# The last 512 tokens of a sliding-window attention: sums transposed straight into the projection's tile, and the load of two constant matrices issued earlier in the spectral layer that follows

## The chip, the cores and the metric

The kernel runs on one core of one Trainium2 chip, with its tensor engine (PE; PEld is its weight load), vector engine (DVE), scalar engine (ACT), GpSimd (POOL) and sync engine (SP, which here only issues DMAs). The metric is the time of one execution in microseconds of the device; a lower time is better.

## The reference

The input is 2048 tokens of 576 numbers in float32. Two layers alternate, twice each:

```
x = x + A(layernorm(x));  x = x + B(layernorm(x));  x = x + A(layernorm(x));  x = x + B(layernorm(x))

A: q, k, v = x @ wqkv  (32 heads of 18)
   p = softmax(q k^T / sqrt(18)) over the 256 newest tokens up to the query's own
   A = (p v, heads side by side) @ wo
B: X = rfft2(x) * (w_r + i w_i);  B = irfft2(X)
```

The weights are the same in both rounds. So the program holds the code of an attention layer and of a spectral layer twice, in what is called here the first and the second half.

## The kernel before, in words

Matrix products are made in a split form: a number is held as a high and a low part, and three products (high by high, low by high, high by low) replace one. Nothing is scheduled by a tool: each engine runs its instructions in the order in which the Python code writes them, and waits on semaphores. SP is one such queue: a DMA that waits for something holds up every DMA that is written behind it. A DMA also takes one of eight semaphores in turn, and waits until the DMA that last had that semaphore has landed.

**Attention.** The 32 heads are worked in eight groups of four (`n`), and each group's 2048 tokens in 16 blocks of 128; a counter `t` runs over the 128 blocks. Scores go through PSUM tiles `S` and `E`, ACT makes the exponentials (tile `P`), POOL masks them, and `pv` (L830) adds them up, by matrix products with the values, into the PSUM tile `U`: a head's 18 sums and, as the 19th row, the sum of its exponentials. Every fourth block ACT copies `U` to `us` (L835). `norm(n, c)` (L836 to L850) then turns the 512 tokens of chunk `c` on their side (four transposes `tpo`, L840), divides by the 19th column (L843, L845) and writes the result to DRAM: columns 0 to 447 of a token into `o_d`, columns 448 to 575 into `o7_d`. Group 7 has columns 504 to 575, group 6 columns 432 to 503.

**Projection.** The class `Out` multiplies by `wo` and adds the input. It works in 16 *units*: unit `u` is the tokens `16 p + u`, one for each partition `p`. So the last 512 tokens are partitions 96 to 127 of every unit. `load(u)` fetches a unit's first 448 columns (into `o`, three buffers) and its input (into `x`, five buffers); `tail(u)` splits 64 of the columns on POOL; `turn(u)` transposes them (L506, L507) and copies them out of PSUM; `early(u)` makes the 22 products that need only these columns (L529), `late(u)` the six that need columns 448 to 575, and the sum with the input (two DVE additions, L551), and stores it. These last columns of all units are in one SBUF tile `o7` of 128 partitions by 16 units by 128 columns, which `last` fetches from `o7_d` (L497); `turn_last` transposes one unit's part (L518, PSUM tile `tpl`), `split_last` copies and splits it (L523 on ACT, L524 on DVE, into `oL`). Units 0 to 2 have their early products while the attention ends. `sums(u)` (L558 to L560) and `stats(u)` (L564, L565) make the next layer's layernorm of a unit.

**Spectral layer.** It has three stages. The first, per unit: `f0` normalises (ACT `xn`, L163) and folds the row (POOL, `eo`, `tl`); `f1` transposes (PSUM `tp`, one buffer, shared with the projection's `turn`) and splits it (`et`, L184 on ACT, L185 on DVE, L186 on ACT); `f2` makes the transform along the row (`pf`, L196), `f3` the first part of that along the tokens (`pz`, L209; copied to `ye` by DVE, L211). Units 3 to 15 of the projection are written in between. `norm(u)`, another function of this name, is `sums` and `f0` of a unit. `f3` writes `ye` to DRAM (`yd`, L223). The last three sets of tokens (`n2` of 13, 14, 15) also go by small SBUF-to-SBUF DMAs (L222) into the first tile of the second stage, whose other rows are read back from `yd` (L215). The second stage works in 16 groups `g`: read two groups' rows from `yd` (L264), multiply (`p`, L276), weigh (DVE L280 to L282, POOL L284, L285), multiply back (`pq`, L295), copy (`ze`, L297), store (L309). Its group 0 needs the rows sent by L222, its group 2 a read of `yd` after the write of all 16 sets. The third stage transforms back with two constant matrices, `ga` and `ic` (0.5 and 1.7 MB), which L219 and L218 load into SBUF over the projection's `wo` and transposed tiles; three small memsets (L217) clear the padding of its `z` tiles there.

## Time and profile before

| | |
|---|---|
| time, median of 3 runs | 1618.0 us (1613.05 to 1623.72) |
| the profiled execution: its own time | 1615.73 us |
| its span | 1614.0 us |
| mean granted clock of the tensor engine | 0.974 |
| PE busy | 1514.2 us, 94% of the span |
| DVE, ACT, POOL busy | 976.2, 813.7, 626.0 us |
| attention ends, projection begins | 512 to 540 us (first half), 1321 to 1349 us (second) |
| second stage of the spectral layer begins | 676.2 us, 1484.6 us |

How to read what follows: a row of the timeline has the start, the duration, engine, line, operation, `out<-in`, shapes and count, and in square brackets how long the engine idled before it and what ended that. A row of the chain of waits has start, duration, engine and line; "SPq" is SP's queue. A row of windows has, for a stretch, busy time and count per engine, the granted clock of PE (1.00 is full), the mean busy share of the DMA engines and GB/s. DMAs that write `o7_d` are shown as `o_d`, those that read it as `ofree<-o_d`; `ofree` is the SBUF area that holds `o`, `x`, `o7` and the second stage's tiles, `oroom` the one of `wo`, the transposed tiles, `ic` and `ga`.

### The profile page before, as it was taken

How to read it: one execution, taken by the hardware profiler on the slowest of the kernel's cores; microseconds unless marked ns; L12 is line 12 of the kernel's file. 1: busy time of each engine (PE TensorE's matmuls, PEld its weight loads, DVE VectorE, ACT ScalarE, POOL GpSimd, SP SyncE). 2: the span in 40 equal slices, each digit the busy share in tenths (PEclk: the TensorE clock that was granted, in tenths of full speed). 3: DMA queues.
4: the chain of work that ended last, by engine and by line, in shares of the span. 5: the costliest groups of instructions: out<-in, count | busy, mean ns of one | idle time of the engine just before them, and what ended most of it. 6: DMA issues, size and time to landing. Idle time of an engine off the chain costs nothing.

```text
span 1614.0 us, 38199 instructions
## 1 busy us (share of the span) xinstructions
PE 1514.2 (94%) x13872; PEld 1145.7 (71%) x13872; DVE 976.2 (60%) x3141; ACT 813.7 (50%) x1900; POOL 626.0 (39%) x1028
## 2 busy tenths in 40 slices
PE   7999999999999899789879999999999998997898
PEld 7975666666656799648879756666666567996498
DVE  4337777777773455356743367777777744554567
ACT  5424666666676344224445146666666773442243
POOL 2172344444455233152411723444343552431524
PEclk9999999999999999898989999999999999998999
DMA  6656456555444456666474563554444444666664
GB/s 204 173 184 209 135 151 188 151 164 149 151 126 135 130 186 193 204 208 213 145 229 111 190 209 121 153 152 138 134 131 146 127 133 120 194 197 198 220 212 140
DMA packets 187881, 268.46 MB, mean 166 GB/s; under 512 B 86830, under 2 KB 91950, under 8 KB 186670
## 3 DMA queue, kind: packets, MB, share of 16 engines
q1 hardware_dynamic: 179374, 246.03, 49.7%
q10 hardware_dynamic: 7680, 15.59, 2.7%
q0 software_dynamic: 640, 4.39, 1.0%
q8 instruction: 111, 1.82, 0.5%
q14 instruction: 76, 0.62, 0.1%
HBM read 167.00 MB, written 102.29 MB: 167 GB/s over the span
## 4 chain that ended last, share of the span: by engine, by line
PE 79%; DMA 8%; ACT 3%; DVE 2%; issue 1%; SPq 1%; POOL 1%; POOLq 0%; ACTq 0%; DVEq 0%
PE pj L741 17%; PE E L814 14%; PE U L830 12%; PE S L782 7%; PE ops L529 6%; PE vps L699 4%; PE pi L340 3%; PE pz L209 3%; PE po L361 3%; PE pf L196 3%; DMA yd<-ze 3%; PE tpo L840 2%; DMA o_d<-o 1%; ACT P L815 1%; PE po L365 1%
## 5 line engine op out<-in xcount | busy, mean ns | idle before, releaser
L784 DVE CUSTOM_DVE_ANT_0 jk<-S,mask 128x384 bf16<-128x384 f32 (+2 forms) x1024 | 500.4, 529 | 155.5 <-PE S L782 143.3
L815 ACT ACTIVATE P<-E 128x384 f32<-128x384 f32 (+2 forms) x1024 | 426.2, 471 | 209.5 <-PE E L814 179.4
L817 POOL TENSOR_SCALAR_AFFINE_SELECT P<-P 128x512 f32<-128x512 f32 x256 | 163.0, 637 | 454.1 <-ACT P L815 437.6
L814 PE MATMUL E<-qs,ks 64*128 64x384 f32 (+2 forms) x1024 | 269.1, 433 | 12.3 <-ACT P L815 11.5
L814 PEld LDWEIGHTS E<-qs,ks 64*128 64x128 f32 x1024 | 129.2, 184 | 156.2 <-ACT P L815 93.3
L782 PE MATMUL S<-ks,qs 63*128 63x384 f32 (+2 forms) x1024 | 228.6, 351 | 0.1
L830 PE MATMUL U<-P,vq 128*19 128x128 f32 x5760 | 209.7, 277 | 0.1
L830 PEld LDWEIGHTS U<-P,vq 128*19 128x19 f32 x5760 | 137.2, 99 | 57.2 <-issue 53.9
L741 PE MATMUL pj<-xh,wqh 128*128 128x512 f32 x360 | 153.6, 427 | 1.8 <-ACT vt L703 1.7
L782 PEld LDWEIGHTS S<-ks,qs 63*128 63x128 f32 x1024 | 130.7, 188 | 24.8 <-DVE m L784 13.3
L820 POOL TENSOR_SCALAR_AFFINE_SELECT P<-P 128x512 f32<-128x512 f32 x224 | 142.6, 637 | 0.0
L741 PE MATMUL pj<-xh,wql 128*128 128x512 f32 x360 | 123.7, 418 | 0.0
L529 PE MATMUL ops<-oroom 128*128 128x288 f32 x784 | 114.7, 303 | 5.1 <-DVE oroom L512 3.0
L741 PE MATMUL pj<-xl,wqh 128*128 128x512 f32 x288 | 119.1, 414 | 0.0
L529 PEld LDWEIGHTS ops<-oroom 128*128 128x128 f32 x784 | 107.1, 192 | 7.4 <-DVE oroom L512 4.0
L340 PE MATMUL pi<-oroom 128*128 128x256 f32 (+1 forms) x576 | 78.5, 293 | 15.6 <-ACT oroom L325 15.6
L745 DVE TENSOR_TENSOR sg<-pj,sg 128x512 fp32r<-128x512 f32 x72 | 49.8, 692 | 70.0 <-ACT sg L744 65.0
L741 PEld LDWEIGHTS pj<-xh,wqh 128*128 128x128 f32 x360 | 67.5, 188 | 33.6 <-issue 21.7
L340 PEld LDWEIGHTS pi<-oroom 128*128 128x128 f32 (+1 forms) x576 | 74.6, 191 | 17.2 <-ACT oroom L325 16.5
L784 DVE DVE_READ_ACCUMULATOR2_ANT m<- 128x1 f32 x1024 | 85.3, 83 | 0.0
L741 PEld LDWEIGHTS pj<-xh,wql 128*128 128x128 f32 x360 | 64.0, 188 | 27.1 <-issue 17.7
L165 POOL TENSOR_TENSOR eo<-xn 128x287 f32<-128x287 f32 x32 | 26.1, 817 | 146.5 <-ACT xn L163 135.4
(165 smaller groups left out, 2562.5 us busy)
## 6 DMA issues: line engine op xcount, KB each, us to landing
qk_d<-sg SPq DMA_DIRECT2D x56, 512.0 KB
qs<-qk_d SPq DMA_DIRECT2D x384, 72.0 KB
ks<-qk_d SPq DMA_DIRECT2D x384, 72.0 KB
v_d<-vt SPq DMA_DIRECT2D x32, 304.0 KB
vq<-v_d SPq DMA_DIRECT2D x16, 608.0 KB
yd<-ye SPq DMA_DIRECT2D x32, 290.0 KB
wt<-in_w SPq DMA_DIRECT2D x16, 580.0 KB
x<-ofree SPq DMA_DIRECT2D x32, 288.0 KB
```

The lines of the kernel that those rows point to most:

```text
L340: T.matmul(o, z[:, sl, c, lo:lo + m], mo, start=k == 0, stop=k == 5)
L529: self.nc.tensor.matmul(self.ps[u][n][:, 0:288], x, self.w[p][:, wk * D + n * 288:wk * D + n * 288 + 288], start=first and i == 0, stop=la ...
L699: T.matmul(ps[:, n, 0:288], xT(xk, c), w[:, wk, n * 288:(n + 1) * 288], start=i == 0, stop=i == len(ks) - 1)
L741: T.matmul(box["ps"], w[:, wk], xT(xk, cs), start=s == 0, stop=s == len(ks) - 1)
L745: V.tensor_sub(sg[:, 1], box["ps"], sg[:, 0].bitcast(F32))
L782: T.matmul(ps[:, 0:N], q[b:b + 63, pair, i * 128:i * 128 + 128], k[b:b + 63, pair, lo:hi], start=True, stop=True)
L784: V.tensor_tensor_reduce(out=jk[:, 0:N], in0=ps[:, 0:N], in1=mask[:, 384 - N:384], scale=1.0, scalar=-3e38, op0=ALU.add, op1=ALU.max, accu ...
L814: T.matmul(ps[:, 0:nq], k[b:b + 64, pair, j * 128:j * 128 + 128], q[b:b + 64, pair, j * 128:j * 128 + nq], start=True, stop=True)
L815: A.activation(p[:, hl_, 0:nq], ps[:, 0:nq], AF.Exp, scale=SC)
L817: P.affine_select(out=p[:, :, 0:128], in_=p[:, :, 0:128], pattern=[[0, 4], [1, 128]], compare_op=ALU.is_ge, fill=0.0, base=0, channel_mult ...
L820: P.affine_select(out=p[:, :, 256:384], in_=p[:, :, 256:384], pattern=[[0, 4], [-1, 128]], compare_op=ALU.is_gt, fill=0.0, base=0, channel ...
L830: T.matmul(U[32 * h:32 * h + 19, (i % 4) * 128:(i % 4) * 128 + 128], vts[n][:, j, h], pt[n, j][:, h, (i - j) * 128:(i - j) * 128 + 128], s ...
```

## The change

It has four parts.

1. The last `norm` of the attention, that of group 7 and the last 512 tokens, is no longer made by four 128x128 transposes, a store and a load. Sixteen transposes take every 16th column of `us`, so that each gives the 32 tokens of one unit on 32 partitions (`tpz`); four pairs of DVE instructions on 32 partitions divide and write `o7` directly. `last` now has a column range: rows 96 to 127 of group 6's 56 columns are fetched behind the constants, and rows 0 to 95 two steps before the counter ends.
2. The `norm` of chunk 2 of group 7 is written one block earlier. `turn_last` and `split_last` of units 0 to 2 are written ahead of the early products of unit 2 instead of behind the turn of unit 3.
3. At the start of the spectral layer `load(6)`, `load(7)`, `tail(6)` and `tail(7)` are written earlier, `norm(2)` ahead of `f1(0)`, and `norm(4)` ahead of `f3(0)`.
4. The memsets and the loads of `ic` and `ga` are taken out of `f3` of set 13 and written behind `f1` of set 12, after the projection's last unit.

```diff
@@ in f3
                 nc.sync.dma_start(y_tile(0)[0:8 * FD].rearrange("p a c f -> p a (c f)"), yd[0][0:2, 0:FD].rearrange("a n i f -> (n i) a f"))
-                for z in zs:
-                    V.memset(z.bitcast(F32)[:, :, :, 289:320], 0.0)
-                nc.sync.dma_start(ic.rearrange("p a f -> p (a f)").bitcast(F32), ic_d.rearrange("p a f -> p (a f)").bitcast(F32))
-                nc.sync.dma_start(ga.rearrange("p a j c -> p (a j c)").bitcast(F32), ga_d.bitcast(F32))
@@ the spectral layer's first stage
         norm(1)
+        out.load(6)
         out.tail(5)
         out.unit(3, pp)
+        norm(2)
+        out.load(7)
+        out.tail(6)
         f1(0, hs[0])
-        norm(2)
         out.unit(4, pp)
         f2(0, hs[0])
         out.ahead(5, pp)
         norm(3)
+        out.tail(7)
         for t in range(1, NT - 4):
...
             if t == 1:
+                norm(4)
                 f3(0, hs[0])
                 out.ahead(6, pp)
-                norm(4)
...
         f1(NT - 4, hs[NT - 4])
+
+        for z in zs:
+            V.memset(z.bitcast(F32)[:, :, :, 289:320], 0.0)
+        nc.sync.dma_start(ic.rearrange("p a f -> p (a f)").bitcast(F32), ic_d.rearrange("p a f -> p (a f)").bitcast(F32))
+        nc.sync.dma_start(ga.rearrange("p a j c -> p (a j c)").bitcast(F32), ga_d.bitcast(F32))
@@ Out
-    def last(self, r):
-        self.nc.sync.dma_start(self.o7[r], self.o7v[r])
+    def last(self, r, c):
+        self.nc.sync.dma_start(self.o7[r, :, c], self.o7v[r, :, c])
...
-        if u < NT - 1:
+        if 7 <= u < NT - 1:
             self.load(u + 1)
             self.tail(u + 1)
@@ the attention's end
-                y = t - 4
-                if 0 <= y < NX and y % 4 == 3:
+                y = t - 3 if t == NX - 2 else t - 4
+                if 0 <= y < NX - 1 and y % 4 == 3 and (t != NX - 1):
                     due.append((norm, *divmod(y // 4, 4)))
...
                     out.consts()
+                    out.last(slice(96, 128), slice(0, 56))
+                if t == NX - 1:
+                    out.last(slice(0, 96), slice(0, 128))
...
-            out.last(slice(0, 96))
             out.early(0, [pp.tile([128, 512], F32, tag="S", name=f"ops0_{n}", bufs=3) for n in range(2)], slice(0, 4))
-            norm(NQ - 1, 3)
-            out.last(slice(96, 128))
+
+            for k in range(4):
+                tp = pp.tile([128, 512], F32, tag=("pj", "E")[k // 2], name=f"tpz{k}", bufs=2)[0:32]
+                for a in range(4):
+                    T.transpose(tp[:, 128 * a:128 * a + 128], us[NQ - 1, 3][:, 4 * k + a:512:16], ident)
+                tv = tp.rearrange("p (a h e) -> p a h e", a=4, h=4)
+                rc = wp.tile([128, 4, 4, 1], F32, tag="rc", name=f"rcz{k}", bufs=2)[0:32]
+                V.reciprocal(rc, tv[:, :, :, 18:19])
+                V.tensor_mul(out.o7[96:128, 4 * k:4 * k + 4, 56:128].rearrange("p a (h e) -> p a h e", e=18), tv[:, :, :, 0:18],
+                             rc.to_broadcast([32, 4, 4, 18]))
             out.early(0, None, slice(4, 11))
             out.early(1, ...)
-            out.early(2, ...)
-            out.turn(3, U, A)
-            out.tail(4)
             tp = pp.tile([128, 512], F32, tag="pj", name="tpl", bufs=2)
             for f in (out.turn_last, out.split_last):
                 for u in range(3):
                     f(u, tp[:, 128 * u:128 * u + 128])
+            out.early(2, ...)
+            out.turn(3, U, A)
+            out.tail(4)
```

Three places show what moves. The first is PE's order at the end of the attention, where the last columns of units 0 to 2 are transposed (`tpl`); `ops_S`, `ops_E` are unit 1's early products, `ops_E` with `ops_pj` unit 2's, `U` here is the turn of unit 3. Before:

```order
L529 MATMUL ops_E<-oroom 128x288
L529 MATMUL ops_pj<-oroom 128x288
L506 MATMUL U<-ident,ofree 128x128 x3
L507 MATMUL U<-ident,ofree 128x128
L518 MATMUL tpl<-ident,ofree 128x128 x3
```

And of the change:

```order
L534 MATMUL ops_S<-oroom 128x288
L534 MATMUL ops_E<-oroom 128x288
L523 MATMUL tpl<-ident,ofree 128x128 x3
L534 MATMUL ops_E<-oroom 128x288
L534 MATMUL ops_pj<-oroom 128x288
```

The three transposes now stand between the early products of units 1 and 2, with 22 products and the turn of unit 3 behind them; before, they stood behind all of these.

The second is DVE's order at the start of the spectral layer, from the additions of unit 3 (`ops_8535`, in the change `ops_8559`) to those of unit 4; `et` is the split of `f1(0)`, the rows from BN_STATS to SCALAR_TENSOR_TENSOR are the layernorm of unit 2. Before:

```order
L551 TENSOR_TENSOR ofree<-ofree,ops_8535 128x288 x2
L185 TENSOR_TENSOR et_8574<-tp_8567,et_8574 128x2x256
L558 BN_STATS ofree<-ofree 128x6 x2
L559 BN_AGGR ofree<-ofree 128x2
L564 RECIPROCAL ofree<-ofree 128x1
L565 SCALAR_TENSOR_TENSOR ofree<-ofree 128x1
L551 TENSOR_TENSOR ofree<-ofree,ops_8593 128x288 x2
```

And of the change:

```order
L556 TENSOR_TENSOR ofree<-ofree,ops_8559 128x288 x2
L563 BN_STATS ofree<-ofree 128x6 x2
L564 BN_AGGR ofree<-ofree 128x2
L569 RECIPROCAL ofree<-ofree 128x1
L570 SCALAR_TENSOR_TENSOR ofree<-ofree 128x1
L185 TENSOR_TENSOR et_8617<-tp_8610,et_8617 128x2x256
L556 TENSOR_TENSOR ofree<-ofree,ops_8621 128x288 x2
```

The four rows of unit 2's layernorm now stand ahead of `et`; on ACT the root, `xn` and the copy to `eo` of unit 2 stand ahead of `et`'s two copies in the same way. One step later the layernorm of unit 4 has moved ahead of the copy `ye` and of unit 6's copies in the same manner.

The third is SP's queue at the end of the spectral layer's first stage. `yd<-ye` are the stores of sets 10, 11, 12 and on, `icr` and `gar` the two constant matrices, `ofree<-yd` the read into the first tile, `ofree<-ye` the small DMAs of set 13. Before:

```order
L223 DMA yd_8484<-ye_9830 16x8x580
L143 DMA wt_9920<-in_w 128x2x580
L223 DMA yd_8484<-ye_9918 16x8x580
L156 DMA m_8496<-in_m 128x1024
L223 DMA yd_8484<-ye_9966 16x8x580
L215 DMA ofree<-yd_8484 104x2x580
L218 DMA oroom<-icr 128x3480
L219 DMA oroom<-gar 128x1024
L222 DMA ofree<-ye_10013 8x580 x2
```

And of the change:

```order
L219 DMA yd_8506<-ye_9852 16x8x580
L260 DMA oroom<-icr 128x3480
L261 DMA oroom<-gar 128x1024
L143 DMA wt_9947<-in_w 128x2x580
L219 DMA yd_8506<-ye_9945 16x8x580
L156 DMA m_8518<-in_m 128x1024
L219 DMA yd_8506<-ye_9993 16x8x580
L215 DMA ofree<-yd_8506 104x2x580
L218 DMA ofree<-ye_10040 8x580 x2
```

The two loads have moved ahead by four DMAs and the read: a load of weights, two stores of `ye`, and the load of `m`.

## The prediction
> **What bounds the kernel now.** I read the page first, then the chain of waits at the two places that the change touches, then the timelines of single engines there and the windows with the granted clock.

> ```profile
> PE 1514.2 (94%) x13872; PEld 1145.7 (71%) x13872; DVE 976.2 (60%) x3141; ACT 813.7 (50%) x1900; POOL 626.0 (39%) x1028
> ```

> PE is busy for 94% of the span, so a microsecond is to be had only where PE stands still or runs at half clock. At the end of the attention the chain of waits of the first half is

> ```profile
> 523.44 5.64 DMA o_d<-o
> 529.10 3.13 DMA ofree<-o_d
> ```

> that is: the last chunk is stored, and then its rows are read back. PE's timeline shows how much of it PE feels, DVE's what follows:

> ```profile
> 529.10 0.49 PE L506 MATMUL U<-ident,ofree 128*128 128x128 f32 x3
> 529.42 0.27 PE L507 MATMUL U<-ident,ofree 128*128 128x128 f32 x1
> 532.48 0.52 PE L518 MATMUL tpl<-ident,ofree 128*128 128x128 f32 x3 [2.78 <-DMA ofree<-o_d]
> 539.71 3.99 PE L529 MATMUL ops<-oroom 128*128 128x288 f32 x28 [1.27 <-DVE oroom L512]
> ...
> 562.87 0.52 PE L506 MATMUL tpo<-ident,ofree 128*128 128x128 f32 x3 [2.07 <-DMA ofree<-o_d]
> ```

> ```profile
> 530.35 0.56 DVE L512 TENSOR_TENSOR oroom<-U,oroom 128x384 fp32r<-128x384 f32 x1 [8.03 <-ACT oroom L511]
> ...
> 534.79 0.81 DVE L551 TENSOR_TENSOR ofree<-ofree,ops 128x288 f32<-128x288 f32 x2
> ```

> The second half stands the same way:

> ```profile
> 1341.20 0.52 PE L518 MATMUL tpl<-ident,ofree 128*128 128x128 f32 x3 [2.83 <-DMA ofree<-o_d]
> ...
> 1371.70 0.52 PE L506 MATMUL tpo<-ident,ofree 128*128 128x128 f32 x3 [2.06 <-DMA ofree<-o_d]
> ...
> 1376.79 0.33 PE L179 MATMUL tp<-ident,eo 128*128 128x128 f32 x1 [0.25 <-DVE oroom L524]
> ```

> At the second place, the step from the spectral layer's first stage to its second, PE stands longer:

> ```profile
> 676.20 4.13 PE L276 MATMUL p<-ofree,fc 128*64 128x290 f32 x16 [6.60 <-DMA ofree<-ye]
> 680.26 1.42 PE L295 MATMUL pq<-uv,m 64*128 64x290 f32 x8
> 683.97 2.15 PE L276 MATMUL p<-ofree,fc 128*64 128x290 f32 x8 [2.29 <-DMA ofree<-yd]
> ...
> 1484.61 4.13 PE L276 MATMUL p<-ofree,fc 128*64 128x290 f32 x16 [7.26 <-DMA ofree<-ye]
> 1488.68 1.69 PE L295 MATMUL pq<-uv,m 64*128 64x290 f32 x8
> 1491.75 1.20 PE L276 MATMUL p<-ofree,fc 128*64 128x290 f32 x8 [1.39 <-DMA ofree<-yd]
> ```

> From the last `ye` on, the chain there is a small DMA, SP's issue, the store of set 15, and the read of groups 2 and 3:

> ```profile
> 670.43 5.30 DMA ofree<-ye
> 675.75 0.58 SPq L223
> 676.44 3.16 DMA yd<-ye
> ...
> 1478.19 5.82 DMA ofree<-ye
> ```

> The small DMA moves 18 KB and takes 5.30 us, in the second half (the last row) 5.82. What holds it and its neighbours is seen on SP: `ic` is issued six microseconds ahead of it, and SP itself waits for it (semaphores are taken in turn), with the stores of sets 14 and 15 queued behind:

> ```profile
> 664.76 0.34 SPq L218 DMA_DIRECT2D oroom<-icr  x1
> ```

> ```profile
> SPq L222 <- DMA oroom<-icr: 3.2, 1, 3.2
> ```

> **Part by part: `ic` and `ga` earlier.** What the small DMA costs alone is seen a stage later, where rows of `ze` go the same way:

> ```profile
> 725.58 0.56 SPq L305
> ```

> ```profile
> 728.73 0.67 ACT L325 CAST oroom<-ofree 128x578 fp32r<-128x578 f32 x1 [6.12 <-DMA ofree<-ze]
> ```

> The last one is issued at 725.58 and its reader runs at 728.73: 3.1 us. I take this; the other bound is today's 5.30. Set 15's leaves at 670.43, so group 0 starts at 673.5 and not at 676.20. From there to the end of the first `pq` it is 681.68 - 676.20 = 5.5 us, which places group 2 at 679.0. The other thing group 2 needs is the read:

> ```profile
> 667.92 0.76 DVE L211 COPY ye<-pz 128x580 f32<-128x580 f32 x1
> ```

> Set 14 is ready at 668.68. SP then issues two small DMAs (0.56 each) and set 14's store (0.58), so set 15's store starts at 670.4 where it started at 676.44; 6.0 us earlier, the read lands for a start at 678.0. The later of the two, 679.0, counts: 5.0 us in the first half. In the second, group 0 starts at 1478.19 + 3.1 = 1481.3, and to the end of `pq` it is 1490.37 - 1484.61 = 5.8, so group 2 stands at 1487.1 and not at 1491.75: 4.65. Bounds per half: nothing (the small DMA still takes 5.3) and 6.0 (the read alone sets it). The second stage goes on in steps that PE and the stores set, so I let the gain pass through whole. **Sum -9.65.**

> The loads themselves now run from about 649. The cover is

> ```profile
> 649.00:664.00 15.00, 13.34 (x101) 12.89 (x100) 6.77 (x10) 6.64 (x13) 2.24 (x5) 1.00 0.47 141
> ```

> DMA engines are 53% idle over these 15 us. The 2.3 MB, issued at 664.76 today, have landed when the small DMA has, at 675.73: 11 us at most, so by 660. Queued behind on SP stand a load of weights, the stores of sets 11 and 12, a load of `m` and the read of the first tile, which today goes just ahead of 664.76; so I let nothing there turn late. The three memsets sit on DVE, 55% idle over that window (6.77 of 15): nothing.

> **The join.** Removed: PE's wait of 2.78 us. Added on PE ahead of the turn of unit 3: 16 transposes less 4, and the three of `tpl`. Three transposes take 529.42 - 529.10 = 0.32, 0.11 each; 15 make 1.65. Their stationary operand now steps by 16 numbers, for which no row exists; bounds 0.09 (a shorter weight load) and, from the slowest row of its kind, below among the rivals. The four DVE pairs handle 288 numbers per partition each, as one of L551's two additions does in 0.4; 0.8 for a pair makes 3.2, beside 36 products of units 0 and 1 at 3.83/28 = 0.137 (unit 3's row less its drain), 4.9. The splits of `tpl` lie beside the 22 of unit 2. So L512 on `U` ends at 530.91 + 1.65 = 532.56, and with it the additions of unit 0 may start, which started at 534.79. From there to unit 3 the chain is DVE's own (additions, statistics, additions, turn of unit 4) and keeps its 4.92 us: unit 3 starts 2.2 us earlier. **-4.5 for both halves**; bounds 2.8 and nothing per half.

> PE then stands, between the late products and unit 3, for about 2.7 us with four transposes in it, longer than today's 1.27. What such a stretch costs:

> ```profile
> 533.90:537.30 3.40, 3.32 (x14) 2.96 (x14) 2.83 (x10) 0.82 (x5) 0.00 (x0) 0.50 0.23 87
> 564.50:567.90 3.40, 3.40 (x17) 3.40 (x16) 1.52 (x3) 2.22 (x5) 3.27 (x9) 0.52 0.10 37
> 1373.00:1376.40 3.40, 3.40 (x27) 3.30 (x25) 1.35 (x3) 2.35 (x5) 3.27 (x8) 1.00 0.24 88
> ```

> After the gap of 2.78 the clock is at half for 3.4 us (at 533.90, hidden there behind DVE); after 2.07 in the first half too (564.50), after 2.06 in the second not (1373.00). I take one halving in the two halves, at unit 3, 3.4 us at half speed: **+1.6**; bounds 0 and 3.2. [...]

> **The start of the spectral layer.** Two layernorms are put ahead of copies that PE waits for.

> ```profile
> 545.62 0.81 DVE L558 BATCH_NORM_STATS2 ofree<-ofree 128x6 f32<-128x288 f32 x2
> 547.91 0.97 PE L196 MATMUL pf<-dc,et 128*128 128x290 f32 x6
> 548.34 0.20 ACT L166 COPY eo<-xn 128x2 f32<-128x2 f32 x1
> ```

> A layernorm from its statistics to the copy of `eo` takes 548.54 - 545.62 = 2.9 us, ACT and DVE in turn. Today only the additions of unit 3 stand between that unit's end (543.70) and `et` of set 0. Now it is 0.81 for them, 2.9, and 0.6 and 0.7 for ACT's and DVE's part of `et` (as in the rows further down): 5.0 us, under a cover of 4.2 (547.91 - 543.70, unit 4). DVE's part is 0.8 late, ACT's, with which `pf` begins, 0.1: I take 0.65 per half, **+1.3**; bounds 0.1 and 0.8. Behind it stand `yh` of set 0 and unit 5's copies on the same engines.

> ```profile
> 556.99 0.69 DVE L185 TENSOR_TENSOR et<-tp,et 128x512 fp32r<-128x512 f32 x1 [0.46 <-ACT et L184]
> 558.95 0.59 ACT L511 CAST oroom<-tpo 128x512 fp32r<-128x512 f32 x1 [0.86 <-PE tpo L509]
> 560.46 0.29 DVE L524 TENSOR_TENSOR oroom<-tpo,oroom 128x128 fp32r<-128x128 f32 x1 [0.33 <-ACT oroom L523]
> ```

> `load(7)`'s wait, 2.07 and 2.06, goes away with its tail's 0.16, since SP issues it behind `xn` of unit 2, ten microseconds ahead of need. Next late is the one PSUM buffer `tp`: unit 6's copies, which started at 558.95, now stand behind unit 4's layernorm: 557.68 + 2.9 = 560.6, 1.65 later, and end at 562.4 instead of 560.75. So the turn of unit 7 moves from 562.87 only to 562.4: with the 0.16, 0.6 per half, **-1.2**. The wait of 0.25 for the next `tp` grows to about 0.7 in the second half, **+0.45**. In the first half it is hidden today under the half clock of unit 6:

> ```profile
> 563.75 5.49 PE L529 MATMUL ops<-oroom 128*128 128x288 f32 x28
> ...
> 1372.58 3.96 PE L529 MATMUL ops<-oroom 128*128 128x288 f32 x28
> ```

> Of these 1.5 us, 1.1 are gained if the shorter gap leaves the clock: **-1.1**.

> **Sum.** -9.65 - 4.5 + 1.6 + 1.3 - 1.2 + 0.45 - 1.1 = -13.1 us. The profiled execution took 1615.73, so 1602.6; it lies 2.3 below the median, and on the median of 1618.0 the forecast is **1605**.

> **Rivals.** *Half of the second stage's gain stays away.* Group 0 comes 2.7 earlier, but group 2 is still late by a wait on the reads or on SP: 5.4 and not 9.65, 1609. For it: 2.29 and 1.39 of PE's waits there are for the read. Against: the read's own chain moves 6.0. Chance 0.17.

> *The load of rows 0 to 95 becomes the wait.* `tpl` now comes two microseconds sooner than its data's old place; that load's landing is hidden today behind the second one's. It is issued earlier, with chunk 2's store. Today the turn of unit 3 begins at 529.10, behind 22 products of unit 2 (3.0); `tpl` now stands ahead of these and behind the transposes, at 529.10 - 3.0 + 1.65 = 527.7. At the worst the data land at 532.2 as now; then 22 products (3.0) and the turn still follow, and unit 3 starts 2 us later than today instead of 2.2 earlier: 1613.5. Against: the second load, a third of the bytes, takes 3.13. Chance 0.06.

> *No half clock, and the read alone sets group 2*: 1.6, 1.0 and 1.35 more, 1601. Chance 0.17.

> *The sixteenths are slow* (the other side). The transposes read `us` in steps of 16 numbers on the path from the attention's last copy to unit 3. The forecast has 6.5 us of gain per half; 16 transposes use it up when each takes 0.11 + 6.5/16 = 0.52 us. At 0.6 it is 1620.6. Against: no row shows a transpose near it; the three above take 0.11. Chance 0.05.

> **Chances and range.** The forecast itself has 0.55, between 1601 and 1608. Less than 1%, 16 us, can't be told from no change here. Under 1601.8 lies most of the third rival and the lower edge of the forecast, moved by the spread of the runs (1613.05 to 1623.72): 0.25. Over 1634 lies a part of the last: 0.03. The range from 1597 to 1613 takes in all cases but the last, with about 4 us of spread on either side.

> **What would show it.** Right: `tpl` without a DMA wait; `ic` and `ga` issued near 649 and SP's L222 not waiting for them; set 15's small DMA near 3.1 us, group 2 some 5.5 us behind group 0 (today 7.8 and 7.1); the turn of unit 7 waiting 1.5 to 2 for unit 6's copies. Wrong: sixteen transposes over 3 us; a clock of 0.5 in both units 3; a second stage that starts early and ends where it ended.

## The result, and the profile after

The changed kernel took 1599.94 us (median of 4 runs, 1593.20 to 1603.07) beside 1619.52 us for the kernel before (4 runs, 1613.05 to 1623.72): a ratio of 0.9877, 95% interval 0.9829 to 0.9925. A second measurement beside more runs of the kernel before (the last experiment) gave 1598.46 against 1615.38, ratio 0.9901, interval 0.9879 to 0.9922. The profiled execution took 1602.12 us, its span is 1600.4; before it was 1615.73 and 1614.0. One profile against the other the change is worth 13.6 us.

PE's line of the page shows that its work is the same; only the span around it is shorter:

```profile
PE 1513.1 (95%) x13896; PEld 1146.8 (72%) x13896; DVE 979.4 (61%) x3153; ACT 813.8 (51%) x1900; POOL 625.7 (39%) x1028
```

PE's timeline at the end of the first half's attention and at the start of its spectral layer (start, duration, instruction, in brackets the idle time before it and what ended it; a line of the kernel before is now 5 higher for the most part, L529 is L534):

```profile
520.57 1.33 PE L534 MATMUL ops<-oroom 128*128 128x288 f32 x8
521.73 1.91 PE L946 MATMUL tpz<-ident,us 128*32 128x128 f32 x16
...
528.27 0.55 PE L523 MATMUL tpl<-ident,ofree 128*128 128x128 f32 x3
...
537.95 5.51 PE L534 MATMUL ops<-oroom 128*128 128x288 f32 x28 [1.27 <-DVE oroom L517]
...
562.58 0.55 PE L511 MATMUL tpo<-ident,ofree 128*128 128x128 f32 x3 [1.51 <-DVE oroom L529]
...
567.88 0.33 PE L179 MATMUL tp<-ident,eo 128*128 128x128 f32 x1 [0.81 <-DVE oroom L529]
```

The sixteen transposes take 1.91 us, `tpl` waits for no DMA any more, unit 3 (537.95) takes 5.51 us, with a granted clock of 0.50 from 538.59 to 542.00, and the turn of unit 7 waits 1.51 us, now for DVE's part of unit 6's copies. In the second half unit 3 takes 3.98 us, at full clock:

```profile
1338.95 3.98 PE L534 MATMUL ops<-oroom 128*128 128x288 f32 x28 [1.27 <-DVE oroom L517]
```

At the step between the spectral layer's stages, the same view of both halves:

```profile
673.96 3.32 PE L281 MATMUL p<-ofree,fc 128*64 128x290 f32 x16 [3.98 <-issue]
677.21 1.88 PE L300 MATMUL pq<-uv,m 64*128 64x290 f32 x8
679.02 1.20 PE L281 MATMUL p<-ofree,fc 128*64 128x290 f32 x8
...
1471.98 4.14 PE L281 MATMUL p<-ofree,fc 128*64 128x290 f32 x16 [4.02 <-DMA ofree<-ye]
1476.05 1.82 PE L300 MATMUL pq<-uv,m 64*128 64x290 f32 x8
1477.80 1.20 PE L281 MATMUL p<-ofree,fc 128*64 128x290 f32 x8
```

PE's first wait is 4.0 us in both halves (6.60 and 7.26 before), the second one, for the read (2.29 and 1.39), is gone. Among SP's waits between 640 and 690 us none is for `ic` any more. SP's and ACT's queues show why: `ic` goes out at 648.03, and set 15's two small DMAs, which ACT issues, leave from 670.81 on; by the semaphores' records the first landed at 673.76, and group 0 starts at 673.96, 3.15 us behind its issue (the first half's row names nothing that ended the wait; the second half's names these DMAs):

```profile
648.03 0.40 SPq L260 DMA_DIRECT2D oroom<-icr  x1
```

```profile
670.81 2.01 ACTq L218 DMA_DIRECT2D ofree<-ye  x2
```

### The profile page after: what moved, and what is told of

Its sections match the earlier page's. It is cut to its first block, busy times and chain, and to the rows that moved or that the text cites. A ratio compares the mean times of both kernels' runs of the same rounds, so it can differ in the third digit from the quotient of the medians.

```text
span 1600.4 us, 38253 instructions
## 1 busy us (share of the span) xinstructions
PE 1513.1 (95%) x13896; PEld 1146.8 (72%) x13896; DVE 979.4 (61%) x3153; ACT 813.8 (51%) x1900; POOL 625.7 (39%) x1028
## 3 DMA queue, kind: packets, MB, share of 16 engines
q1 hardware_dynamic: 179278, 245.44, 49.9%
## 4 chain that ended last, share of the span: by engine, by line
PE 79%; DMA 6%; ACT 3%; DVE 3%; POOL 2%; issue 1%; SPq 1%; POOLq 0%; ACTq 0%; DVEq 0%
PE pj L746 15%; PE E L819 14%; PE U L835 12%; PE S L787 6%; PE ops L534 6%; PE pi L345 4%; PE vps L704 4%; DMA yd<-ze 3%; PE po L366 3%; PE pf L196 3%; PE pz L209 3%; PE tpo L845 2%; PE p L281 1%; PE po L370 1%; PE pq L300 1%
## 5 line engine op out<-in xcount | busy, mean ns | idle before, releaser
L534 PE MATMUL ops<-oroom 128*128 128x288 f32 x784 | 113.9, 301 | 4.4 <-DVE oroom L517 3.0
L534 PEld LDWEIGHTS ops<-oroom 128*128 128x128 f32 x784 | 106.7, 191 | 6.2 <-DVE oroom L517 4.0
L345 PEld LDWEIGHTS pi<-oroom 128*128 128x128 f32 (+1 forms) x576 | 74.8, 192 | 18.8 <-ACT oroom L330 17.8
```

Of the source, the lines that this page charges most:

```text
L345: T.matmul(o, z[:, sl, c, lo:lo + m], mo, start=k == 0, stop=k == 5)
L534: self.nc.tensor.matmul(self.ps[u][n][:, 0:288], x, self.w[p][:, wk * D + n * 288:wk * D + n * 288 + 288], start=first and i == 0, stop=la ...
```

## Experiments

The theory is the sum of the prediction: the loads are worth most, the join some 2 us per half, the start of the spectral layer nothing. Its rivals are that the join or chance in the clock carries the gain, or that a gain is given back a step later. Two distances on PE's timeline are used throughout, since they hold less chance than the whole time: from the end of the last `pz` to the end of the last `pq` (the second stage with its step), and from the first early product (520.57 above) to unit 3 (537.95).

**The two loads alone.** In the kernel before, the memsets and the loads of `ic` and `ga` are moved behind `f1` of set 12:

```diff
             if n2 == FD:
                 nc.sync.dma_start(y_tile(0)[0:8 * FD]...)
-                for z in zs:
-                    V.memset(z.bitcast(F32)[:, :, :, 289:320], 0.0)
-                nc.sync.dma_start(ic..., ic_d...)
-                nc.sync.dma_start(ga..., ga_d...)
...
         f1(NT - 4, hs[NT - 4])
+        (the same four lines)
```

> Only the loads of ic and ga, with the memsets, are moved, from the step of set 13 to behind the last unit; all else is as before. If the step between the spectral layer's stages is worth what the sum says, PE waits about 4 us there instead of 6.6 to 7.3, group 2 of the second stage follows group 0 by about 5 us instead of 7.8 and 7.1, and the time falls by 9 to 10 us, three quarters of the whole gain. If the whole gain comes from the join or from fewer stretches at half clock, the wait is shorter but the time falls by less than 5 us.

1602.33 us against 1614.37, ratio 0.9916 (0.9887 to 0.9944). PE's timeline at the step:

```profile
671.90 3.86 PE L276 MATMUL p<-ofree,fc 128*64 128x290 f32 x16 [4.00 <-issue]
675.69 1.36 PE L295 MATMUL pq<-uv,m 64*128 64x290 f32 x8
676.98 1.20 PE L276 MATMUL p<-ofree,fc 128*64 128x290 f32 x8
```

The wait is 4.00, group 2 comes 5.1 us behind group 0, as in the whole change. The medians differ by 12 us where 9 to 10 were expected; the interval (9 to 18 us) holds these. The loads carry most of the gain.

**The join alone.** In the kernel before, only the order of the attention's last sums, `last`, the sixteen transposes and the place of `tpl` are those of the change:

```diff
-            out.last(slice(0, 96))
             out.early(0, ..., slice(0, 4))
-            norm(NQ - 1, 3)
-            out.last(slice(96, 128))
+            for k in range(4):
+                (four transposes of us, reciprocal, product into o7)
...
+            (tpl: turn_last and split_last of units 0 to 2)
             out.early(2, ...)
             out.turn(3, U, A)
             out.tail(4)
-            (tpl: turn_last and split_last of units 0 to 2)
```

> Only the join is changed (the last chunk transposed straight into the projection's tile, the last columns ahead of unit 2's early products); loads and layernorms stay as before. By the sum, unit 3 starts about 2.5 us earlier per half against the first early products, so the time falls by 3 to 5 us; where PE's stretch ahead of unit 3 halves the clock, 1.5 us of that is lost in that half. If the transposes' place is filled by another wait, unit 3 starts where it did and the time is the same within 1 us.

1608.21 us, ratio 0.9957 (0.9936 to 0.9978). From the first early product to unit 3 it is 18.5 and 17.8 us, where the kernel before has 19.9 and 20.1. In the first half the load of rows 0 to 95 shows:

```profile
529.12 0.55 PE L518 MATMUL tpl<-ident,ofree 128*128 128x128 f32 x3 [0.98 <-DMA ofree<-o_d]
...
538.80 5.20 PE L529 MATMUL ops<-oroom 128*128 128x288 f32 x28 [1.27 <-DVE oroom L512]
```

so a rival of the prediction exists, at 1 us and not 4; over all kernels with the join `tpl` waits for it in eight of fourteen halves, 0.21 to 0.98 us. Unit 3 (538.80) took 5.20 us here and 5.51 in the second half: both at half clock by their length (3.98 us at full clock), which the prediction had as a sign against it. The medians differ by 6 us where 3 to 5 were expected, while the two distances give 1.4 and 2.3 us and half clock takes back 1.2 and 1.5; what the rest of these 6 us is, the profile doesn't show.

**The start of the spectral layer alone.** In the kernel before, the loads and tails of units 6 and 7 and `norm(2)` and `norm(4)` stand where the change has them:

```diff
         norm(1)
+        out.load(6)
         out.tail(5)
         out.unit(3, pp)
+        norm(2)
+        out.load(7)
+        out.tail(6)
         f1(0, hs[0])
-        norm(2)
...
             if t == 1:
+                norm(4)
                 f3(0, hs[0])
                 out.ahead(6, pp)
-                norm(4)
```

> Only the start of the spectral layer is changed: the loads of units 6 and 7 and the layernorms of units 2 and 4 stand earlier. By the sum the two cancel nearly: the turn of unit 5 comes 0.6 us later per half, the turn of unit 7 0.6 us earlier, so the time is the same within 2 us. If the removed wait for the load of unit 7 were worth its whole 2.2 us per half, it would fall by 4 us or more.

1613.16 us, ratio 0.9996 (0.9976 to 1.0017): the same, as the sum had it. PE waits 1.5 us at the turn of unit 7 and 0.8 behind it:

```profile
1366.82 0.55 PE L510 MATMUL tpo<-ident,ofree 128*128 128x128 f32 x3 [1.50 <-DVE oroom L528]
...
1372.12 0.33 PE L179 MATMUL tp<-ident,eo 128*128 128x128 f32 x1 [0.81 <-DVE oroom L528]
```

The three parts together make 0.0131 of the time, about 21 us, with wide intervals; the whole makes 0.0099 to 0.0123.

**The layernorms put back.** The changed kernel, with `norm(2)` again behind `f1(0)` and `norm(4)` behind `ahead(6)`; `load(7)` and `tail(6)` follow `norm(2)`, since the load overwrites what it reads.

```diff
-        norm(2)
-        out.load(7)
-        out.tail(6)
         f1(0, hs[0])
+        norm(2)
+        out.load(7)
+        out.tail(6)
...
-                norm(4)
                 f3(0, hs[0])
                 out.ahead(6, pp)
+                norm(4)
```

> The changed kernel, but with the layernorms of units 2 and 4 back behind the copies that PE waits for; the loads stay early. By the theory that the layernorms ahead of the copies cost PE 0.6 us at the turn of unit 5 and 1.5 us at the turn of unit 7, both go: unit 7 turns right behind the second product of set 1, and the time falls by 2 to 4 us against the changed kernel. By the rival that some later copy, or the next layernorm, is then the late one, PE waits as much a step later and the time is the same within 1 us.

1599.12 us, ratio 0.9902 (0.9872 to 0.9931), against 0.9877 and 0.9901 for the changed kernel: the same. The timeline shows the rival:

```profile
557.62 0.55 PE L511 MATMUL tpo<-ident,ofree 128*128 128x128 f32 x3
...
564.75 0.33 PE L179 MATMUL tp<-ident,eo 128*128 128x128 f32 x1 [2.65 <-DVE oroom L529]
```

The turn of unit 7 no longer waits, and the transposes of set 2 behind it wait 2.65 us instead of 0.81, for unit 7's copies, which now stand behind `norm(4)`. From unit 3 to there it is 28.23 us in the second half, 28.44 in the changed kernel: of 2.1 us removed 0.2 remain. ACT and DVE, not their order, set the pace there.

**The loads on another queue.** The kernel before with the loads at their old place, issued by ACT:

```diff
-                nc.sync.dma_start(ic..., ic_d...)
-                nc.sync.dma_start(ga..., ga_d...)
+                nc.scalar.dma_start(ic..., ic_d...)
+                nc.scalar.dma_start(ga..., ga_d...)
```

> The kernel before, with the loads of ic and ga at their old place in the program but issued by ACT, so that SP no longer waits for ic's semaphore; the bytes move at the same time as before. If SP's wait was what held group 2, the stores of sets 14 and 15 go out about 4 us earlier, PE's second wait there (2.3 and 1.4 us for the read) goes, and the time falls by 3 to 4 us; the small DMA of set 15 still takes over 5 us, so PE's first wait stays at 6.6 to 7.3 us. If the bytes in flight were the whole cause, both waits and the time stay as before within 1.5 us.

1609.63 us against 1615.09, ratio 0.9962 (0.9946 to 0.9979). SP's queue, who it waited for, and ACT's queue:

```profile
667.03 1.29 SPq L222 DMA_DIRECT2D ofree<-ye  x2
674.28 1.26 SPq L223 DMA_DIRECT2D yd<-ye  x2
```

```profile
SPq L223 <- DMA ofree<-yd: 10.3, 2, 5.9
```

```profile
671.97 2.98 ACTq L222 DMA_DIRECT2D ofree<-ye  x2
```

SP no longer waits for `ic`, but for the read of the first tile, issued at the same moment as `ic` and now the late one: 5.9 us at most. The stores of sets 14 and 15 leave at 674.28, 6.4 us behind the last `pz` (6.15 before, at 675.75). ACT's two small DMAs leave at 671.97, 4.1 us behind the last `pz`, where they left 0.8 behind it before (670.43). So the wait did not go: it moved. ACT's first small DMA takes the semaphore that `ic` had, and leaves 0.10 us after `ic` has landed (671.87 by the semaphores' records in the trace; in the second half 1478.04, and the small DMA leaves at 1478.11); group 0 then starts 3.4 us later, at 675.37. The second stage with its step takes 51.0 and 49.9 us.

So this run doesn't separate a wait for `ic`'s semaphore from slow transfers beside its bytes. The trace of the kernel before does. There set 13's first small DMA leaves before SP stands still (669.98 to 673.18), and the changed kernel's chain has set 14's with nothing large ahead of it:

```profile
665.63 0.74 SPq L222 DMA_DIRECT2D ofree<-ye  x1
```

```profile
669.11 2.02 DMA ofree<-ye
```

Before, set 13's landed at 674.88, 9.25 us after its issue, and set 14's, issued at 669.35, at 675.95, 6.60 us after; in the changed kernel set 14's took 2.02. So in the kernel before the bytes in flight make group 0 late, without SP's wait for `ic`.

The time of this run fell all the same, which neither theory had, so it was run again:

> The kernel before with the two loads issued by ACT, a second time. Its first profile showed the step between the stages as long as before (51.0 and 49.9 us from the last pz to the last pq), yet its time was 5.5 us lower. If that gain lies in the step, this profile shows the step shorter by 2 us or more per half; if it lies in stretches at half clock elsewhere, the step is the same within 1 us and the times come nearer to those before.

1610.37 against 1615.38, ratio 0.9969 (0.9953 to 0.9984), the step 50.6 and 49.6 us. Over both profiles the step is 0.7 us per half below that of the kernel before (50.3 against 51.0), less than the latter's own spread (50.0 to 52.3); where the other 4 us lie is not shown, and stays open.

**The loads later still.** The changed kernel with the four lines behind the last set:

```diff
         f1(NT - 4, hs[NT - 4])
-        (memsets, loads of ic and ga)
         for t in range(NT - 4, NT + 1):
             ...
+        (memsets, loads of ic and ga)
```

> The changed kernel with the loads of ic and ga (and the memsets) moved on behind the last set instead of ahead of it, so that they are issued behind the small DMAs and stores of sets 14 and 15. If only what is issued behind the loads is held by them, group 0 starts 4.0 us after the last pz as in the changed kernel, but the reads of the groups 4 and on stand behind 2.3 MB, PE waits some 3 to 6 us at group 4, and the time is 2 to 8 us above the changed kernel. If any two transfers at the same time slow each other whatever their order, group 0 is late too (over 5 us after the last pz).

1609.06 us, ratio 0.9965 (0.9945 to 0.9986): the loads' gain is gone. SP's queue and PE:

```profile
666.24 0.58 SPq L265 DMA_DIRECT2D oroom<-icr  x1
667.00 0.72 SPq L266 DMA_DIRECT2D oroom<-gar  x1
669.75 16.75 SPq L270 DMA_DIRECT2D ofree<-yd  x6
```

```profile
668.55 1.25 PE L282 MATMUL p<-ofree,fc 128*64 128x290 f32 x8 [4.25 <-DMA ofree<-ye]
673.11 2.20 PE L282 MATMUL p<-ofree,fc 128*64 128x290 f32 x8 [3.30 <-issue]
675.24 1.80 PE L301 MATMUL pq<-uv,m 64*128 64x290 f32 x8
677.99 1.20 PE L282 MATMUL p<-ofree,fc 128*64 128x290 f32 x8 [0.95 <-DMA ofree<-yd]
```

Group 0, whose DMAs left a microsecond or more ahead of the loads, is on time (4.25); what comes behind pays, at group 1 already (3.30) and again at the read: 50.3 and 53.6 us for the stage. The row of group 1 names nothing that ended its wait, but its last rows come by set 15's second small DMA, which ACT issues:

```profile
666.49 0.66 ACTq L218 DMA_DIRECT2D ofree<-ye  x1
```

That is 0.25 us behind `ic` (666.24), on the other queue; by the semaphores' records it landed at 673.02, 6.5 us later, and group 1 starts at 673.11. In the second half it left 0.19 us ahead of `ic` (1467.56 and 1467.75) and still took 5.3 us, while set 15's first one, 1.1 and 1.0 us ahead of `ic`, took 3.3 and 3.1. So what was issued behind the 2.3 MB (6.5 us), or just ahead of them (5.3 us), was held here, on another queue than theirs; a lead of 1.1 and 1.0 us was enough. The price was 9 to 11 us above the changed kernel's two medians, not 2 to 8, and it fell due at groups 1 and 2, not 4.

**Keeping PE busy.** The changed kernel, with 30 transposes that nobody reads ahead of the second stage and 70 ahead of the third:

```diff
+        def fill(n, name):
+            tp = pp.tile([128, 2, 512], F32, tag="tp", name=name, bufs=1)
+            for k in range(n):
+                T.transpose(tp[:, 0, 128 * (k % 4):128 * (k % 4) + 128], ident, ident)
+        fill(30, "fila")
...
         pipe(16, [(9, g2), (7, g1m), (2, gw), (0, g0)])
+        fill(70, "filb")
```

> The changed kernel with transposes that nobody reads put where PE stands still: 30 of them (30 x 0.109 = 3.3 us) between the first and the second stage of the spectral layer, 70 (7.6 us) between the second and the third. If TensorE's clock for each stretch of 3.41 us is set by how busy PE was in the stretch before, both stages now begin at full clock: the first two groups of the second stage take 2.9 us instead of 5.1 to 5.8, the first pi 4.6 instead of 7.3, and the time falls by 5 to 10 us against the changed kernel. If the half clock there is set by something else, or is hidden behind waits for ACT and for DMAs, the time is the same within 1.5 us. If the transposes run into the work that follows, it is slower.

1596.73 us against 1615.09, ratio 0.9894 (0.9876 to 0.9913): no change against 0.9901. PE's timeline:

```profile
670.98 2.25 PE L290 MATMUL p<-ofree,fc 128*64 128x290 f32 x16 [0.72 <-issue]
673.81 1.50 PE L309 MATMUL pq<-uv,m 64*128 64x290 f32 x8 [0.58 <-POOL uv L298]
675.60 1.20 PE L290 MATMUL p<-ofree,fc 128*64 128x290 f32 x8 [0.29 <-DMA ofree<-yd]
...
695.28 1.20 PE L290 MATMUL p<-ofree,fc 128*64 128x290 f32 x8 [1.15 <-ACT ze L311]
```

What the clock theory had for the two stages came: with the transposes ahead of them both begin at full clock (group 0 and 1 in 2.25 us instead of 3.32 and 4.14, the first 36 products `pi` of the third stage in 5.1 instead of 7.2), and of the 34.3 us that the granted clock takes from the changed kernel (each stretch by what it lacks to 1) 15.0 are left, at a mean granted clock of 0.991 instead of 0.979. But the time doesn't follow: the stage takes 45.1 and 45.3 us instead of 45.6 and 46.2, because PE then waits for POOL's sums, for the read, and longer for ACT's copies `ze` (1.15 us, in the second half 1.69). From the last `pz` to the end of the third stage it is 126.0 us in both halves, beside 126.4 to 127.6 in the changed kernel's two profiles: half clock there is hidden for the most part.

**Keeping it busy in four more places.** As before this, and 9 transposes ahead of unit 3, 12 ahead of the turn of unit 7 and 12 between the transposes and the products of set 12 (these two written into free columns of a tile in use), and 90 at the end of the first half:

```diff
             out.turn(4, ...)
+            (9 transposes into a free tile)
...
             f2(t, hs[t])
+            if t == 1: (12 transposes into out.tp[:, 1, 256:512])
             out.ahead(u + 2, pp)
...
         def f2(n2, h):
+            if n2 == NT - 4: (12 transposes into h["tp"][:, :, 384:512])
...
         pipe(NT, [(0, ly), (4, i1), (5, i2), (2, i0)])
+        (in the first half: fill(90, "filc"))
```

> As the kernel before this one, and with transposes that nobody reads also ahead of unit 3 (9), ahead of the turn of unit 7 (12), between the transposes and the products of set 12 (12), and at the end of the first half (90). By the clock theory no stretch at half clock is left in the spectral layer, and the time falls by a further 1 to 5 us, since each of these places halved the clock in only some of the runs (1.5 us each); by the rival it is the same or up to 2 us slower, by what the transposes hold up.

1605.72 us, ratio 0.9945 (0.9930 to 0.9959): 9 us slower than the kernel before it. Two of the fillers share a tile with copies, and so wait for these and only then run:

```profile
561.78 1.53 PE L263 MATMUL tpo<-ident 128*128 128x128 f32 x12 [1.51 <-DVE oroom L548]
...
650.83 1.58 PE L194 MATMUL tp<-ident 128*128 128x128 f32 x12 [2.61 <-ACT et L189]
```

From unit 3 to the last `pz` that is 133.1 and 133.2 us, where the kernel before it has 130.4 and 129.1; the filler at the end of the half moved the next attention's first transposes from 10.8 to 13.1 us behind the last `po`, because DVE's first instruction there waits for it:

```profile
806.67 0.06 DVE L621 MEMSET eps<- 128x1 f32 x1 [8.49 <-PE filc L279]
```

These three differences (2.7, 4.1 and 2.3 us) make up the 9 us. Unit 3 shows what was meant, 3.95 us in both halves, though chance gives that too. So this run prices careless fillers, and doesn't tell what good ones at those places would give.

**The two kernels once more.**

> The changed kernel once more, for a closer interval beside the parts. If the parts add up (loads alone 0.9916, join alone 0.9957, start alone 0.9996 of the time before), the whole is at 0.987, some 21 us below the kernel before; by the sum of the prediction it is 13 us, 0.992. In its profile a second placing of the stretches at half clock: at unit 3 in one of the two halves, if it is chance.

> The kernel before once more, for a second profile of it on the same chip: from the last pz to the last pq 50 to 52 us per half, and stretches at half clock at other places than in the first profile.

The changed kernel: 1598.46 us (6 runs), ratio 0.9901 (0.9879 to 0.9922), 16 us; the parts had said 21, the sum 13, and the interval (12.6 to 19.5 us) holds the 13; the 21, with a wide interval of its own, lies just outside. Unit 3 ran at full clock in the first half this time and at half in the second (3.98 and 5.45 us). The kernel before: 1608.99 in its one run; the stage takes 51.2 and 50.5 us. Over all profiles:

| last `pz` to last `pq`, us, first and second half | |
|---|---|
| before | 52.3, 50.0 |
| before, again | 51.2, 50.5 |
| join alone | 50.2, 49.9 |
| start alone | 49.9, 52.7 |
| loads alone | 45.4, 46.1 |
| changed | 45.6, 46.2 |
| changed, again | 45.7, 46.3 |
| layernorms back | 45.4, 45.5 |

The mean is 50.8 with the loads at the old place and 45.8 at the new one; the two don't overlap. From the first early product to unit 3 it is 20.0 us (18.7 to 21.1) in the twelve halves without the join and 17.8 (17.3 to 18.5) in twelve with it, the kernel with four fillers left out.

## Why the prediction was right

The forecast was 1605 us on the median and 1602.6 for the profiled execution, which took 1602.12; the median came out at 1599.94, within the range. That the one profiled execution came within 0.5 us is luck: the four executions spread over 10 us, and the median lies 5 us under the forecast and below the 1601 to 1608 that the prediction gives the forecast itself. The rival at 1601 is nearer in number, but its mechanism did not come: there is half clock at unit 3, and in the changed kernel group 2 doesn't wait for the read. Term by term:

- **`ic` and `ga`, -9.65.** 5.0 us per half in the table, 10.0 in all. The steps hold too: group 0 starts 3.15 us behind the issue of its small DMA and 4.0 us behind the last `pz`, group 2 stands 5.1 and 5.8 us behind group 0 (forecast 5.5 and 5.8), no wait for the read, and the gain passes through the stage. The loads themselves have landed at 656.6 (forecast by 660). One thing was read wrongly without harm: before, group 0's last rows were not set 15's (landed at 675.73) but set 14's (675.95), held in the same way. What the step from group 0 to 2 consists of was not seen then: with the fillers it takes 4.6 us in the first half, since part of it is half clock.
- **The join, -4.5.** 20.0 - 17.8 = 2.2 us per half, 4.4 in all. The strided transposes take (1.91 - 0.27) / 15 = 0.109 us each, no more than contiguous ones (0.11), so the rival on the slow side has no ground.
- **The clock at unit 3, +1.6.** Half clock in one half of two in both profiles of the changed kernel, and in 6 of the 12 halves of the kernels with the join (the one with four fillers left out): 5.2 to 5.5 us instead of 3.98. In the twelve halves without the join there is none (3.98 to 4.00 us), so it comes with the join, whose longer stretch the prediction had as the reason; which half pays differs between the two profiles of the changed kernel. What stood ahead of these stretches is shown below.
- **Start of the spectral layer.** `norm(2)`, +1.3: from unit 3 to the turn of unit 5 it is 1349.59 - 1338.95 = 10.64 us in the second half, 10.09 before, so +0.55 per half (forecast 0.65). The turn of unit 7 waits 1.51 (forecast 1.5 to 2), the next transposes 0.81 (forecast 0.7). Unit 6 takes 3.96 us in both halves, so the -1.1 came as well, and not by luck: unit 6 is at half clock (5.17 to 5.50 us) in 6 of the 12 halves whose kernels lack this part, and in none of the 10 that have it as in the change, with a wait of 1.5 instead of 2.1 us ahead of it (four fillers left out). So the change takes away one place that pays 1.5 us in half of the cases, and the join adds another. The part alone is worth nothing that can be measured, as summed.
- **The rivals.** Half of the second stage's gain staying away: it didn't. The load of rows 0 to 95: a wait in eight of fourteen halves, 1 us at most; the forecast of 532.2 for its landing was the old place of another load.

Where the sum is short of the measured 16 to 20 us can't be told term by term: both intervals reach down to between 12 and 13, and half clock moved by chance between the profiles (41.7 us taken from the kernel before, 34.3 from the changed one, but about 35 in the second profile of the kernel before, by its mean granted clock of 0.978 over 1607.3 us). The second half's attention, from the last `po` to the first early product, which the change hardly touches, took 520.5 to 526.4 us in the profiles; so one profile beside another can't settle 6 us.

## What to carry to other kernels

A large load that nobody needs yet should be issued where nothing small and urgent follows it, or leaves in the same microsecond: 2.3 MB ahead of 18 KB cost 5 us per half; another queue shortened the step by 0.7 us, within its spread, a later place by nothing, only an earlier one by all. When a wait is removed, look for the next one on the same chain before counting it: here a layernorm put forward or back moved 2 us between two neighbouring waits and changed nothing, and a stage freed from half clock waited for ACT instead. Compare distances between marks in the traces of several variants; they told 5 us from nothing where the whole time spread over 10.

## What the hardware showed

```profile
535.18:538.59 3.41, 1.60 (x12) 1.13 (x10) 2.55 (x13) 1.33 (x4) 0.00 (x0) 1.00 0.64 235
538.59:542.00 3.41, 3.41 (x17) 3.41 (x16) 1.72 (x6) 1.68 (x4) 1.76 (x4) 0.50 0.73 217
...
647.82:651.23 3.41, 1.74 (x12) 1.30 (x11) 1.77 (x5) 2.23 (x5) 2.24 (x5) 1.00 0.91 287
651.23:654.65 3.42, 3.42 (x17) 3.40 (x17) 0.44 (x1) 0.64 (x1) 0.00 (x0) 0.50 0.96 391
...
668.30:671.71 3.41, 1.68 (x12) 1.44 (x11) 1.52 (x2) 0.00 (x0) 0.00 (x0) 1.00 0.41 106
671.71:675.12 3.41, 1.16 (x10) 0.64 (x11) 0.00 (x0) 0.00 (x0) 0.00 (x0) 1.00 0.64 181
675.12:678.54 3.42, 3.42 (x16) 1.89 (x16) 2.72 (x6) 0.00 (x0) 1.78 (x3) 0.50 0.79 249
```

The windows in which PE is busy for 1.60, 1.74 and 1.16 us of 3.41 are followed by one at half clock; one with 1.68 was not, so these rows show no sharp limit. In these two profiles, cut so, 17 windows at full clock from the end of an attention to the end of the spectral layer are followed by half clock, with 0.00 to 1.74 us of PE; besides the one with 1.68, one with 1.70 in the kernel before (1370.15 to 1373.56) is followed by full clock. Within the attention it is otherwise: there five windows with 2.40 to 2.72 us were followed by half clock too, for which these runs show no reason. Ahead of unit 3 in the first half PE stood for 1.27 and for 0.54 us within one window (535.18 to 538.59), and half clock followed. Where the clock falls differs from run to run (first at 486.10 us in the kernel before, at 487.39 in the changed one, which is no whole multiple of 3.413), and so do the places that pay 1.5 us; two executions of the changed kernel took 1593.20 us at a mean granted clock of 0.987 and 1602.12 at 0.979; 0.008 of 1600 us is 13 us of clock beside 9 us of time.
